# Attention and FFN on one core: k and v loaded in tiles of tokens 8 apart, sums of the first batch from the factors, numerators in two banks

## The chip, the core and the metric

The kernel runs on one core of a Trainium2 chip. The core has five engines that work side by side, each on a queue of its own, in order: TensorE (PE, matrix products; its weight loads are listed as PEld), VectorE (DVE), ScalarE (ACT), GpSimd (POOL) and SyncE (SP, which here only issues transfers). TensorE writes its results to PSUM, a memory of eight banks of 128 partitions x 512 float32; everything else lies in SBUF (128 partitions). Transfers to and from HBM run on 16 DMA engines; an engine issues one and later waits for its landing. The metric is the device time of one execution in microseconds (us), smaller is better: the median of several runs.

## The reference

Two parts, cut to what matters (batch 4, heads 4, sequence 1088, head_dim 32, r = 8, so 64 features; FFN of 128 x 2048 over 4352 tokens):

```python
def phi(x):
    a = np.einsum('rd,bhsd->bhsr', S1, x)
    b = np.einsum('rd,bhsd->bhsr', S2, x)
    return np.einsum('bhsi,bhsj->bhsij', a, b).reshape(*x.shape[:-1], r * r)
q_p, k_p = (phi(q), phi(k))
kv = np.einsum('bhsf,bhsd->bhfd', k_p, v)
z = np.sum(k_p, axis=2)
num = np.einsum('bhsf,bhfd->bhsd', q_p, kv)
den = np.einsum('bhsf,bhf->bhs', q_p, z)[..., None] + 1e-06
attn = (num / den)
...
x = attn.transpose(0, 2, 1, 3).reshape(B * S, H * D)
h = np.maximum(x @ w_in, 0.0)
out = h * h @ w_out
```

Each token has two sets of 8 factors, a and b; a feature is a product a_i b_j. The sum z of the features over the tokens can be had from the features (a column of ones beside v), or from the factors: the product of all a with all b over the tokens holds every sum of a_i b_j.

## The kernel before

The work is one long FFN with the attention of later batches woven in. The 1024 main tokens of a batch form two groups of 512 (four tiles of 128 each), and 64 tokens are left over ("rest"). So there are eight chunks of 512 tokens and one chunk of 256 rest tokens. A chunk passes through 16 blocks: `first_product` (line 892) multiplies a 128-column slice of w_in with xT into a `pg` bank (tag "pg", two banks), Relu and Square follow on VectorE and ScalarE (or ScalarE and GpSimd, or ScalarE alone), and `block` (973) multiplies the result with w_o into `po`. `store_gen` (862) turns `po` back, scales it with beta and writes it out. A float32 product is recorded as two instructions.

The order is written out by hand. Attention of batches 1 to 3 is made of generators in `lanes`, which `pump` advances after each block by block numbers and rough engine loads; `later` lists loads by block number. The first group of batch 0 has nothing to hide behind, and its code stands in order from line 1004 on:

- s_ps turns S1 and S2; w_bd is made of it on VectorE.
- `turned` (246) transposes 32x32 blocks of k and q on VectorE; `proj` (269) makes the factors of four tiles in TensorE (16 recorded instructions a tile group) and ScalarE copies them.
- `outer` (340) makes features from the factors, half of a group on VectorE, half on GpSimd.
- `Kv` (389) multiplies features of k with v and a column of ones, four heads a tile, into kv_ps; `finish` copies it to kvbd, the block-diagonal right side, with the sums in column 32 of each block.
- `turned_half` (1050) transposes features of q in TensorE (`t_ps`, tag "ms", two banks) and copies them to phTh; the second group's (phq1) go by `turn_features` directly: two tiles a time for both `t_ps`.
- `numerators` (527) multiplies them with kvbd into nd, one PSUM tile of two banks (tag "nd", one buffer); `normalize` (544, with parts=4) divides on VectorE and makes xs (float16); x_ps transposes xs to xT.
- `first_two` (931) issues the first two `pg`; the second group's numerators follow, then the gapless run of blocks.

`idle_products` (237) are products of zeros that keep TensorE going in its waits. Batches 1 to 3 have their sums from the factors already (`KvRows`, 428), with constants made in a lane (`sum_constants`, 220).

Loads are issued from SP in the order of lines 164 to 184; k of batch 0 by group (`load_k`, 95), v by head (`load_v`, 121, one a head), v's rest in two. In SBUF partition 32h + j of k holds 34 neighbouring tokens of head h; the transposes write with a stride of four so that tile t has every token of its place.

Of the kernel before, what the change touches and what calls it, by code (L numbers as in the profile page):

```python
# [21 lines left out]
def kernel(  # L22
# [32 lines left out]
    Identity = mybir.ActivationFunctionType.Identity  # L55
# [33 lines left out]
    def load_all(t, src, b):  # L89
        sp.dma_start(  # L90
            t[:, :],
            bass.AP(src.tensor, src.offset + b * H * S * D, [[NM * D, 128], [1, NM * D]]),
        )

    def load_k(b, g):
        sp.dma_start(
            _v(k_sb[b], 128 * g, [[256, 4], [1, 128]]),
            bass.AP(
                k.tensor,
                k.offset + b * H * S * D + 128 * g,  # L100
                [[NM * D, 128], [256, 4], [1, 128]],
            ),
        )
# [9 lines left out]
    def load_rest(t, src, b):  # L113
        sp.dma_start(
            t[:, 1024:1088],
            bass.AP(
                src.tensor, src.offset + b * H * S * D + 1024, [[NM * D, 128], [1, 64]]
            ),
        )

    def load_v(b, h, eng):
        eng.dma_start(
            v_sb[b][:, 256 * h : 256 * h + 256],
            bass.AP(
                v.tensor,
                v.offset + (b * H + h) * S * D,
                [[NM * D, 32], [8 * D, 4], [1, 256]],
            ),
        )

    def load_v_rest(b, i, eng):
        eng.dma_start(
            _v(v_rm[b // 2], 0, [[D, H], [1, D]], 64 * (b % 2) + 32 * i, 32),
            bass.AP(
                v.tensor,
                v.offset + (b * H * S + 32 + i) * D,
                [[NM * D, 32], [S * D, H], [1, D]],
            ),
        )
# [25 lines left out]
    load_k(0, 0)  # L165
    load_k(0, 1)
    load_rest(k_sb[0], k, 0)
    load_q(0, 0)
    for i in range(4):
        load_v(0, i, sp)  # L170
    load_q(0, 1)
    for i in range(2):
        load_v_rest(0, i, sp)
# [3 lines left out]
    load_all(k_sb[1], k, 1)  # L177
    load_w_o(1)
    for i in range(4):
        load_v(1, i, sp)  # L180
    for i in range(2):
        load_v_rest(1, i, sp)
    load_all(q_sb[1], q, 1)
    load_rest(q_sb[0], q, 0)


# [5 lines left out]
    eps = cpool.tile([128, 1], F32)  # L192
    dve.memset(eps[:], 1e-6)
# [26 lines left out]
    def sum_constants():  # L220
        yield 1, 0
        dve.tensor_reduce(
            out=pick_s[:, :], in_=_v(iden, 0, [[1, 32], [32, 4]]), axis=AX, op=add
        )
        yield 1, 0
        pool.tensor_copy(
            out=_v(pick, 0, [[8, 32], [1, 8]]), in_=_v(pick_s, 0, [[1, 32], [0, 8]])
        )
        dve.tensor_reduce(
            out=_v(own_j, 0, [[8, 2], [1, 8]]),  # L230
            in_=_v(iden, 0, [[64, 2], [1, 8], [8, 8]]),
            axis=AX,
            op=add,
        )

# [10 lines left out]
    def turned(x, g, of_q=False):  # L246

        if g < 2:
            xt = apool.tile([128, 512], F32, tag="xt", bufs=6)
            c0, w = (512 * g, 128) if of_q else (128 * g, 256)  # L250
            dve.transpose(  # L251
                _v(xt, 0, [[128, 4], [1, 4], [4, 32]]), _v(x, c0, [[32, 4], [w, 4], [1, 32]])
            )
        else:
            xt = apool.tile([128, 64], F32, tag="xtr", bufs=4)
            if of_q:
                dve.transpose(_v(xt, 0, [[1, 2], [2, 32]]), _v(x, 1024, [[32, 2], [1, 32]]))
            else:
                dve.transpose(xt[:, :], x[:, 1024:1088])
# [9 lines left out]
    def proj(xt, ps_tag="ms"):  # L269
# [5 lines left out]
        act.copy(ab[:, :], ab_ps[:, :])  # L275
# [64 lines left out]
    def outer(ph, ab, t0, m, eng, a=None, g=None):  # L340


        if g is None:
            a, b, n, c0, c1 = ab if a is None else a, ab, 16, 64 * t0, 64 * t0 + 8
        else:
            a, b, n, c0, c1 = ab, ab, 8, 128 * g + 32 * t0, 256 + 128 * g + 32 * t0
        eng.tensor_tensor(  # L347
            out=_v(ph, 256 * t0, [[64, 4 * m], [8, 8], [1, 8]]),
            in0=_v(a, c0, [[n, 4 * m], [1, 8], [0, 8]]),
            in1=_v(b, c1, [[n, 4 * m], [0, 8], [1, 8]]),  # L350
# [37 lines left out]

    class Kv:

        def __init__(self, b):
            self.b, self.n = b, 0
            self.ps = pspool.tile([128, 512], F32, name="kv_ps", tag="nd", bufs=1)

        def products(self, ph, c0, vt, v0, v1, one, p0=0, n=128):
            z = 64
            for h in range(H):
                off = v0 + v1 * h
                for f in range(0, 64, z):
                    x = 64 * (h % 2) + f  # L400
                    nc.tensor.matmul(  # L401
                        self.ps[x : x + z, 64 * (h // 2) : 64 * (h // 2) + 64],
                        ph[p0 : p0 + n, c0 + 64 * h + f : c0 + 64 * h + f + z],
                        _v(vt, off, [[one - off, 2], [1, D]], p0, n),
                        start=self.n == 0 and h < 2,
                        stop=False,
                        skip_group_check=True,
                    )
            self.n += 1

        def tiles(self, ph, g, ts):
            for t in ts:
                self.products(ph, 256 * t, v_sb[self.b], D * (4 * g + t), 256, VONE)

        def rest(self):
            r, p0 = self.b // 2, 64 * (self.b % 2)
            self.products(rest_ab[r][1], 0, v_rm[r], 0, D, H * D, p0, 64)

        def finish(self, engs):
            u = self.b  # L420
            for x in range(2):
                evict(
                    engs[x],
                    _v(kvbd[u], VW * x, [[2 * VW, 2], [1, VW]], 64 * x, 64),
# [729 lines left out]
```

## Time and profile before

| what | value |
| --- | --- |
| runs | 198.64, 198.82, 198.88 us; median 198.82 |
| the profiled execution | 199.0 us, of it the span of the trace 197.2 us |
| VectorE, ScalarE, GpSimd busy | 61%, 57%, 32% of the span |
| a block (`pg` and the two passes of `po`) | starts 1.07 us apart |
| transfers | 21.91 MB, mean 111 GB/s, over 300 GB/s from 9.3 to 20.6 us |
| k transposes of batch 0 | 3.90 to 6.01 us |
| first kv product | 9.29 us |
| first numerators of group 0 | 13.90 us |
| first `pg` / first `po` | 19.04 / 21.09 us |

The span runs from the first to the last instruction of the trace; the run's time has some 1.8 us more around it. In the rows of a timeline the columns are start, length (both us), engine, line, operation, output<-inputs, shapes and count; in brackets stands the engine's idle time before it and what ended it. In a row of a stage the columns are the stage, its length, and the busy time and number of instructions of PE, PEld, DVE, ACT and POOL, then granted clock, DMA share and GB/s.

### The profile page before, as it was taken

The page shows a single profiled execution, that of the slowest core. Times are in us where ns is not written, and L with a number is a line of the kernel's source. Part 1 is how long each engine was busy: PE and PEld are TensorE (multiplying, and loading weights), DVE is VectorE, ACT ScalarE, POOL GpSimd, SP SyncE. Part 2 cuts the span into 40 slices and gives each one's busy share as a digit, 9 for nine tenths or more (in the row PEclk, how much of TensorE's full clock was granted, in tenths as well). Part 3 has the DMA queues.
Part 4 walks back from the last instruction along what each step waited for, and adds up shares of the span by engine and source line. Part 5 has one row for each costly group of instructions (what it writes and reads, how often), then busy time and mean ns, then how long its engine had stood idle before and what let it go on. Part 6 is the DMA issues. An engine that isn't in the chain of part 4 may idle for free.

```text
span 197.2 us, 3669 instructions
## 1 busy us (share of the span) xinstructions
PE 191.5 (97%) x1402; PEld 102.7 (52%) x1402; DVE 120.5 (61%) x264; ACT 112.5 (57%) x221; POOL 64.0 (32%) x84
## 2 busy tenths in 40 slices
PE   7999999999999999999999999999999999999992
PEld 2784544555545454555554645455545444544791
DVE  4837897565587738547977264556387545545671
ACT  3235767663666666464757474557466656565570
POOL 3604224635245018241632271516313222222000
PEclk9999999999999999999999999999999999999999
DMA  5799840395990105982000159721000100100011
GB/s 159 217 341 326 279 128 2 83 269 165 267 327 34 56 3 130 294 240 99 2 5 0 55 118 303 193 98 53 2 0 3 53 0 0 53 0 2 0 57 27
DMA packets 13634, 21.91 MB, mean 111 GB/s; under 512 B 2672, under 2 KB 8048, under 8 KB 13616
## 3 DMA queue, kind: packets, MB, share of 16 engines
q1 hardware_dynamic: 13376, 21.60, 36.6%
q8 instruction: 11, 0.18, 0.4%
q10 hardware_dynamic: 240, 0.07, 0.2%
q14 instruction: 7, 0.06, 0.1%
HBM read 15.61 MB, written 6.06 MB: 110 GB/s over the span
## 4 chain that ended last, share of the span: by engine, by line
PE 94%; DMA 2%; DVE 1%; issue 1%; ACT 0%
PE po L994 56%; PE pg L906 16%; PE nd L265 5%; PE ab_ps L265 3%; PE kvr_ps L438 2%; PE po L953 2%; PE o_ps L871 2%; PE po_r L953 2%; DMA k_sb<-in_k_dram 2%; PE kv_ps L401 1%; PE x_ps L617 1%; PE ab_ps L282 1%; PE t_ps L1042 1%; PE idle_ps L240 1%; PE abr_ps L265 0%
## 5 line engine op out<-in xcount | busy, mean ns | idle before, releaser
L994 PE MATMUL po<-g,w_o 128*128 128x512 f32 x256 | 130.6, 592 | 0.0
L923 DVE TENSOR_SCALAR gt<-pg 128x512 f32<-128x512 f32 (+1 forms) x107 | 69.2, 651 | 52.5 <-PE pg L906 38.1
L926 ACT ACTIVATE g<-gt 128x512 f32<-128x512 f32 (+1 forms) x107 | 63.8, 598 | 58.8 <-DVE gt L923 56.4
L994 PEld LDWEIGHTS po<-g,w_o 128*128 128x128 f32 x256 | 48.5, 191 | 35.7 <-issue 19.2
L914 POOL TENSOR_TENSOR g<-gt 128x512 f32<-128x512 f32 x23 | 23.9, 1040 | 79.3 <-ACT gt L913 79.3
L906 PE MATMUL pg<-xT,w_in 128*128 128x512 f16 x126 | 47.8, 380 | 0.0
L906 PEld LDWEIGHTS <-w_in 128*128 128x128 f16 x142 | 13.8, 98 | 25.0 <-issue 24.1
L332 POOL TENSOR_TENSOR phF<-f,f 128x576 f32<-128x576 f32 (+1 forms) x12 | 16.1, 1364 | 12.8 <-DMA f<-q_two 12.8
L347 POOL TENSOR_TENSOR ph_k<-ab 128x512 f32<-128x512 f32 x14 | 14.5, 1070 | 10.1 <-ACT ab L288 8.8
L913 ACT ACTIVATE gt<-pg 128x512 f32<-128x512 f32 x23 | 13.4, 581 | 0.0
L879 DVE TENSOR_TENSOR o_sb<-o_ps,beta 128x512 f32<-128x512 f32 x8 | 5.5, 692 | 6.9 <-PE o_ps L871 6.9
L251 DVE STREAM_TRANSPOSE xt<-k_sb 128x512 f32<-128x512 f32 x8 | 8.6, 1117 | 1.7 <-DMA k_sb<-in_k_dram 1.7
L265 PEld LDWEIGHTS nd<-kvbd,phF 128*64 128x64 f32 x208 | 6.9, 137 | 4.5 <-issue 4.5
L251 DVE STREAM_TRANSPOSE xt<-q_sb 128x512 f32<-128x512 f32 x8 | 8.6, 1121 | 0.0
L265 PEld LDWEIGHTS ab_ps<-w_bd,xt 128*64 128x64 f32 x160 | 7.1, 163 | 2.5 <-issue 1.2
L265 PE MATMUL ab_ps<-w_bd,xt 128*64 128x64 f32 x160 | 7.5, 252 | 0.4 <-DVE w_bd L1008 0.4
L920 ACT ACTIVATE g<-gt 128x512 f32<-128x512 f32 x12 | 7.6, 630 | 0.4
L240 PE MATMUL idle_ps<-zero 128*128 128x512 f16 x17 | 6.6, 511 | 1.2 <-DVE own L198 1.2
L265 PE MATMUL nd<-kvbd,phF 128*64 128x66 f32 x208 | 7.7, 224 | 0.0
L919 ACT ACTIVATE gt<-pg 128x512 f32<-128x512 f32 x12 | 7.0, 587 | 0.0
L953 PE MATMUL po<-w_o,g 128*128 128x128 f32 x32 | 6.2, 278 | 0.0
L953 PE MATMUL po_r<-w_o,g 128*128 128x128 f32 x32 | 6.0, 275 | 0.0
(114 smaller groups left out, 143.4 us busy)
## 6 DMA issues: line engine op xcount, KB each, us to landing
q_two<-qf SPq DMA_DIRECT2D x8, 288.0 KB, 4.1
f<-q_one SPq DMA_DIRECT2D x4, 576.0 KB, 6.1
f<-q_two SPq DMA_DIRECT2D x4, 576.0 KB, 4.7
v_sb<-in_v_dram SPq DMA_DIRECT2D x16, 128.0 KB, 4.0
out_dram<-o_sb SPq DMA_DIRECT2D x8, 256.0 KB, 2.4
k_sb<-in_k_dram SPq DMA_DIRECT2D x3, 544.0 KB, 6.1
q_sb<-in_q_dram SPq DMA_DIRECT2D x3, 544.0 KB, 4.4
w_in<-in_moe_w_in_dram SPq DMA_DIRECT2D x2, 512.0 KB, 6.2
```

The source lines that it names most:

```text
L240: nc.tensor.matmul(idle_ps[:, :], zero[:, 0:128], zero[:, :])
L251: dve.transpose(_v(xt, 0, [[128, 4], [1, 4], [4, 32]]), _v(x, c0, [[32, 4], [w, 4], [1, 32]]))
L265: nc.tensor.matmul(out_ps[p0 + c : p0 + c + z, c0 : c0 + w], lhsT[:, l0 + c : l0 + c + z], rhs)
L332: pool.tensor_tensor(out=ph[:, c], in0=fs[g][0][:, c], in1=fs[g][1][:, c], op=mult)
L347: eng.tensor_tensor(out=_v(ph, 256 * t0, [[64, 4 * m], [8, 8], [1, 8]]), in0=_v(a, c0, [[n, 4 * m], [1, 8], [0, 8]]), in1=_v(b, c1, [[n, 4 ...
L906: nc.tensor.matmul(pg[:, 0:nt], w_in[:, 128 * c : 128 * c + 128], xT[:, 0:nt])
L913: act.activation(gt[:, 0:nt], pg[:, 0:nt], Relu)
L914: pool.tensor_tensor(out=g2[:, 0:nt], in0=gt[:, 0:nt], in1=gt[:, 0:nt], op=mult)
L923: dve.tensor_scalar(out=gt[:, 0:nt], in0=pg[:, 0:nt], scalar1=0.0, scalar2=None, op0=amax)
L926: act.activation(g2[:, 0:nt], gt[:, 0:nt], Square)
L953: nc.tensor.matmul(po[r][:, 0:128], g2[:, 128 * r : 128 * r + 128], w_o[:, 128 * c : 128 * c + 128], start=c == 0, stop=c == NC - 1,)
L994: nc.tensor.matmul(po[0][:, 0:nt], w_o[:, 128 * c : 128 * c + 128], g2[:, 0:nt], start=(c == 0), stop=(c == NC - 1),)
```

## The change

*Loads.* k lies by head: partition 32h + j holds, for t = 0 to 3, the tokens 256t + 8j to 256t + 8j + 7 of head h. That is one load a head into 32 partitions (for batch 0 the fourth from ScalarE's queue), and one for the rest. v is one load a batch, its rest one. The transposes then write contiguously, and a tile's tokens are 8 apart. A chunk's rows are written out by four transfers of 32 partitions instead of one of 128.

*Sums of batch 0.* The column of ones is gone from `Kv`; `factor_sums` multiplies the factors, ScalarE copies the result (kvz), `pick_sums` and `own_sums` bring it into kvbd, as `KvRows` did for the others. The constants are made at the start.

*Order and numerators.* w_bd comes before the k transposes; an idle product stands between the two projections of k. All eight q transposes follow the kv products. The first group's numerators go to two tiles (nd and nd_b, the latter with the tag "pg"), with the second group's projection between. `normalize_first` takes both: ScalarE copies the fourth tile's numerators (num_last), VectorE makes three tiles of xs, GpSimd the fourth. The second group's features are turned in two halves, its second half and the numerators of it behind `first_two`; the last numerators come in a lane (`second_half`), behind the second `po`. ScalarE converts w_in in 2 + 2 pieces, not 3 + 1.

Cut to its core:

```diff
-    def load_k(b, g):
-        sp.dma_start(
-            _v(k_sb[b], 128 * g, [[256, 4], [1, 128]]),
+    def load_k(b, h, eng):
+        eng.dma_start(
+            _v(k_sb[b], 0, [[256, 4], [1, 256]], 32 * h, 32),
             bass.AP(
                 k.tensor,
-                k.offset + b * H * S * D + 128 * g,
-                [[NM * D, 128], [256, 4], [1, 128]],
+                k.offset + (b * H + h) * S * D,
+                [[8 * D, 32], [256 * D, 4], [1, 8 * D]],
             ),
+        )
...
+    def load_v(b):
+        sp.dma_start(
+            _v(v_sb[b], 0, [[256, H], [1, 256]]),
             bass.AP(
+                v.tensor, v.offset + b * H * S * D, [[8 * D, 128], [S * D, H], [1, 8 * D]]
             ),
         )
...
-    load_k(0, 0)
-    load_k(0, 1)
-    load_rest(k_sb[0], k, 0)
+    for h in range(H):
+        load_k(0, h, act if h == 3 else sp)
+    load_k_rest(0)
     load_q(0, 0)
-    for i in range(4):
-        load_v(0, i, sp)
+    load_v(0)
...
+    def factor_sums(ps, c0, ab, a0, a1, w, p0, n, first, last):
+
+        nc.tensor.matmul(
+            ps[32 * w : 32 * w + 32, c0 : c0 + 32],
+            ab[p0 : p0 + n, a0 : a0 + 32],
+            ab[p0 : p0 + n, a0 + a1 : a0 + a1 + 32],
+            start=first,
+            stop=last,
+        )
...
             for h in range(H):
-                off = v0 + v1 * h
-                for f in range(0, 64, z):
-                    x = 64 * (h % 2) + f
...
+                x = 64 * (h % 2)
+                nc.tensor.matmul(
+                    self.ps[x : x + 64, D * (h // 2) : D * (h // 2) + D],
+                    ph[p0 : p0 + n, c0 + 64 * h : c0 + 64 * h + 64],
+                    vt[p0 : p0 + n, v0 + v1 * h : v0 + v1 * h + D],
...
+    def normalize_first(nds, xT):
...
+        act.copy(_v(last, 0, [[32, 4], [1, 32]]), _v(nds[1], 256, [[VW, 4], [1, 32]]))
+        for i, nd in enumerate(nds):
+            dve.tensor_reduce(
+                out=_v(top, 8 * i, [[4, 2], [1, 4]]),
+                in_=_v(nd, 0, [[256, 2], [VW, 4], [1, 32]]),
+                axis=AX, op=amax, apply_absolute_value=True,
+            )
+            dve.tensor_scalar(
+                out=den[:, 8 * i : 8 * i + 8], in0=_v(nd, D, [[256, 2], [VW, 4]]),
+                scalar1=1e-6, scalar2=None, op0=add,
+            )
...
+        for t in range(3):
+            dve.scalar_tensor_tensor(
+                out=_v(xs, 128 * t, [[32, 4], [1, 32]]),
+                in0=_v(nds[t // 2], 256 * (t % 2), [[VW, 4], [1, 32]]),
...
+        pool.tensor_tensor(
+            out=_v(xs, 384, [[32, 4], [1, 32]]),
+            in0=_v(last, 0, [[32, 4], [1, 32]]),
+            in1=_v(rs, 12, [[1, 4], [0, 32]]),
+            op=mult,
+        )
...
-        sp.dma_start(dst, o_sb[:, :])
+        for dst, p0, n, c0, w in dsts:
+            sp.dma_start(dst, _v(o_sb, c0, [[1, w]], p0, n))
...
-    xk = [turned(k_sb[0], 0)]
     dve.tensor_tensor(
         out=_v(w_bd, 0, [[16, H], [1, 16]]),
...
+    xk = [turned(k_sb[0], 0), turned(k_sb[0], 1)]
...
+    pk = [proj(xk[0], "pg")]
+    idle_products(1)
+    pk.append(proj(xk[1], "pg"))
...
+    for g in range(2):
+        for t in range(4):
+            factor_sums(kv0.ps, 512, pk[g][1], 32 * t, 128, t, 0, 128, g == 0, g == 1 and t > 0)
+    factor_sums(kv0.ps, 512, rest_ab[0][0], 0, 32, 0, 0, 64, False, True)
+    sums = apool.tile([128, 32], F32, name="kvz", tag="kvz")
+    act.copy(sums[:, :], kv0.ps[:, 512:544])
...
+    idle_products(2)
+    kv0.tiles(phk[0], 0, range(4))
+    zt_ps = pspool.tile([128, 32], F32, name="zt_ps", tag="po", bufs=2)
+    pick_sums(zt_ps, 0, sums)
+    own_sums(0, zt_ps, 0)
+    xq1 = turned(q_sb[0], 1, True)
...
-    kv0.tiles(phk[1], 1, range(4))
+    kv0.tiles(phk[1], 1, range(2))
     kv0.rest()
+    kv0.tiles(phk[1], 1, range(2, 4))
     kv0.finish((act, act))
-    turned_half(2, (act, dve))
+    pqT = [turned_half(phq, 0, (act, act)), turned_half(phq, 2, (act, dve))]
+    nd0 = [numerators(0, pqT[0], None, range(2))]
     pq1 = proj(xq1, "pg")
     phq1 = ph_tile("ph_q", 2)
     outer(phq1, pq1[1], 0, 2, pool)
-    nd0 = numerators(0, pqT)
+    nd_b = pspool.tile([128, 512], F32, name="nd_b", tag="pg", bufs=2)
+    nd0.append(numerators(0, pqT[1], nd_b, range(2, 4)))
     idle_products(2)
...
+    norm = normalize_first(nd0, xT0)
     next(norm)
+    outer(phq1, pq1[1], 2, 2, pool)
+    for c in range(2):
...
+    pqT = [turned_half(phq1, 0, (act, act))]
+    idle_products(4)
+    chunk_of(0, 0, xT0, next(norm))
     first_two()
-    nd1 = numerators(0, pqT1, True)
+    nd1 = numerators(0, pqT[0], None, range(2))
+    pqT.append(turned_half(phq1, 2, (act, dve)))
     nd_taken[0] = True
     for _ in range(2):
         first_product()
...
+    def second_half():
+        numerators(0, pqT[1], nd1[:, 512:1024], range(2, 4))
+        yield 1, 0
+        yield from x_gen(0, 1, None, (), nd1)
+
+    lanes.append([second_half(), 2, 1])
```

## The prediction

> **What bounds the kernel now.** I read the busy times and the chain of waits of the page first, then busy time by stage, then the timeline of the first 28 us, then the loads.
>
> ```profile
> PE 191.5 (97%) x1402; PEld 102.7 (52%) x1402; DVE 120.5 (61%) x264; ACT 112.5 (57%) x221; POOL 64.0 (32%) x84
> ...
> PE 94%; DMA 2%; DVE 1%; issue 1%; ACT 0%
> ```
>
> TensorE is busy for 191.5 of 197.2 us and is 94% of the chain that ended last. By stage:
>
> ```profile
> 14.90:20.64 5.74, 5.35 (x57) 2.86 (x53) 4.32 (x14) 3.65 (x8) 2.25 (x4) 1.00 1.00 327
> 20.64:190.00 169.36, 169.36 (x1137) 87.55 (x1134) 105.71 (x223) 102.48 (x198) 56.79 (x61) 1.00 0.33 96
> ```
>
> From 20.64 us on TensorE has no gap. Its order there is the same before and after, except for what the change pushes into the first blocks. So the question is when the gapless part begins and how much work it must hold. The opening, in order of time (idle time before a row stands in brackets):
>
> ```profile
> 3.90 1.09 DVE L251 STREAM_TRANSPOSE xt<-k_sb 128x512 f32<-128x512 f32 x1 [1.71 <-DMA k_sb<-in_k_dram]
> ...
> 5.09 2.10 PE L265 MATMUL ab_ps<-w_bd,xt 128*64 128x64 f32 x32 [0.41 <-DVE w_bd L1008]
> ...
> 9.29 1.36 PE L401 MATMUL kv_ps<-v_sb,ph_k 128*64 128x64 f32 x32
> ```
>
> The chain runs: first k load (lands at 3.87), transpose, projections, kv products, then the numerators, VectorE's normalisation, x transposes and the first `pg` at 19.04. Some rows of its end:
>
> ```profile
> 12.80 0.66 PE L1042 MATMUL t_ps<-iden,ph_q 128*128 128x128 f32 x4
> ...
> 13.90 0.42 DVE L77 COPY phTh<-t_ps 128x256 f32<-128x256 f32 x1 [2.68 <-ACT phTh L75]
> ...
> 18.40 0.60 PE L1042 MATMUL t_ps<-iden,ph_q 128*128 128x128 f32 x4
> ...
> 21.07 1.29 DVE L923 TENSOR_SCALAR gt<-pg 128x512 f32<-128x512 f32 x2 [0.74 <-PE pg L906]
> ```
>
> Two things matter here. VectorE's copy out of a `t_ps` starts only when ScalarE's copy from the same tile has ended (13.86): two engines' reads of one PSUM tile stand in line. And the four t_ps transposes at 18.40 lie in TensorE's wait for the first xT, so they cost nothing now.
>
> **The change, part by part.** Where I give "before -> after", the first is from the timeline, the second is my running sum.
>
> *Loads of k.* The first transpose reads all 128 partitions, so it now waits for all four head loads instead of the 256 KB of `load_k(0,0)`. The nearest row is the second k load, with which the same 512 KB are in:
>
> ```profile
> DMA to landing us min/median/max: 3.1/3.4/3.6
> ```
>
> It was issued at 1.22 and took 3.4: 4.6. Three issues on SP at about 0.5 each (v issues took 0.59 to 0.67, k issues 0.45 to 0.53) put the third head at 1.8 to 2.0; the fourth stands behind two s_nat issues on ScalarE, at 1.66. With the smallest landing of a 128 KB v load, 2.5, that is 4.4; with 3.6 it is 5.6. I take 4.8. Moving w_bd ahead of the transposes costs nothing, since s_ps is in at 4.14 and w_bd takes 0.20. The two reductions of the constants (0.34, 0.40) fit in VectorE's idle 1.71 before 3.90, the pick copy (0.40) in GpSimd's 3.0 before w_bt. Without that cover each would delay the w_bd line by its length.
>
> [...]
>
> *Projections to kv products.* Turned k at 4.8 + 1.06, TensorE starts at 5.9 (before 5.09). The pace is half in this stage: the idle products at 1.19 are 0.43 apart, those at 16.18 0.21. The 32 projections of k took 1.89 (5.09 to 6.98), so 0.95 to 6.85; the new idle product 0.43 to 7.28; second half 0.95, rest 0.12, q 1.06 (as 7.27 to 8.33): 9.4. The 18 new factor_sums instructions load 32-wide weights. Their pitch at full pace is in these rows of weight loads (first and last columns: start and length; one lasts 0.11 to 0.14):
>
> ```profile
> 120.86 0.49 PEld L438 LDWEIGHTS kvr_ps<-ph_k,v_sb 128*32 128x32 f32 x32 [0.76 <-issue]
> ...
> 123.59 0.32 PEld L485 LDWEIGHTS kvt_ps<-kvz,pick 128*64 128x64 f32 x8
> ```
>
> (0.49 - 0.11)/31 = 0.012 each, double at half pace: 0.2 to 0.45, I take 0.35, to 9.75. Two idle products, 0.43 to 0.86, take 0.6: kv starts at 10.35 (before 9.29). VectorE (k turned to 6.9, q to 8.25, first ph_k to 8.95) and GpSimd (ph_k to 8.4) are done by then, v is in (a 512 KB load issued near 3.3; the old last v quarter, issued at 4.83, landed 3.2 later). The kvz copy (0.19) ends about 10.15, under the idle products.
>
> *kv products.* 72 instructions, with 32 streamed columns instead of 64. The pick row above, 64-wide weights and 16 columns, still has a pitch of (0.32 - 0.138)/7 = 0.026; the numerators' loads (64-wide, 66 columns) have (1.02 - 0.137)/31 = 0.0285. Halving the columns should thus save next to nothing. Before, the two groups took 1.30 and 1.46; 72 x 0.0285 is 2.05. With 8 pick instructions (0.2) the bounds are 2.25 and 2.96, I take 2.6: end at 12.95. Before it was 12.80, but with an idle product and half of the t_ps transposes in between (10.59 to 11.34).
>
> *Turned q features and numerators.* All eight t_ps now follow: 2 x 0.53, to 14.0. ScalarE copies kvbd (0.43) and three phTh (0.375 each) from 13.1 to 14.72, VectorE's follows to 15.17. First numerators from 14.35, 0.5; projection 0.51; second bank 0.5: end at 15.85 (before 14.95).
>
> *Normalisation.* The first bank's reduction and den are hidden. ScalarE's copy num_last (0.26, as the 128x128 xT_rem copy) reads nd_b first, and VectorE's reduction stands behind it: 16.27, reduction 0.42, den 0.17: 16.9. From there to the first xs 1.02 as now (16.13 to 17.15), three xs of 0.28 instead of four, and 0.76 from the last xs to `pg` (18.28 to 19.04): 19.55. GpSimd's share of the fourth tile (0.20 and about 0.4, by the 256-wide product's 0.62) ends before the third xs. So `pg` is 0.5 late. Removing ScalarE's den (0.27) is in this sum.
>
> *After `pg`.* The second half of the next group's t_ps (0.53) and of its numerators (0.55) now stand behind the first two `pg`. The numerators were behind them before too; the transposes were not, so 0.53 enters the gapless part. And a new line forms, counted from `pg`: ScalarE Relu 0.62 to 1.22, Square to 1.86, its phTh to 2.23, VectorE's phTh behind it to 2.69, the next gt to 3.35. TensorE ends its first po at 2.86 and its next `pg` needs that gt's bank: a gap of 0.54. Before, that gt ended at 21.75 and the `pg` went at 22.01, so no gap. The second `pg` of the steady part, 4.04 behind the first one before (23.08), comes at 5.05: 1.0 more.
>
> *SP and the stores.* A store is four issues instead of one (0.54 to 0.64 each, 1.7 more). At 44.12 four factor transfers stand behind the store; the last, issued at 51.29, lands 4.0 to 6.2 later, so with 1.7 more by 59.2, GpSimd's two products (2.8) end at 62.0 and the numerators start at 61.96. Bound 0 to 0.1, I take 0. The last stores (186.40) end their issue before the rows at 193.36. Later k loads are five issues instead of one, v two instead of six: even.
>
> **Sum**: 0.5 + 1.0 = 1.5. The profiled execution took 199.0 (span 197.2 and 1.8 around it), so 200.5; against the median of 198.82 it is **200.3**. Taking the cheap end everywhere (loads 0.4, idle and sums 0.3, kv 0.35, num_last 0.3, no gap 0.54) gives -0.4; the dear end (loads 0.8, 0.36, 0.36) 3.0.
>
> **Rivals.** [...] *B, kv products cost by their columns*: they then halve, 1.0 less, 199.3. The pick row speaks against it. *C, not slower*: TensorE's full pace comes before the projections, at about 6 us rather than 9.5. Then they and the idle products shrink, and kv starts when VectorE's first ph_k ends, 8.85 instead of 10.35: all of the 1.5 is gone, 198.8. It decides only if TensorE counts as busy enough across its longer gap, now 4.69 to 5.9; the old gap, to 5.09, did not bring it. [...] *D, the change doesn't do what it says in time*: the two lines I see behind ScalarE do not cost what I charge, and the split pays: no gap after `pg` (0.54), num_last out of the way (0.3) and kv at its cheap end (0.35) leave 1.5 - 1.2 = 0.3: 199.1. For it: VectorE is busy for 4.32 of the 5.74 us up to 20.64, so it has some room; against: the wait for ScalarE in the row at 13.90.
>
> **Numbers.** Forecast 0.50 (199.6 to 201.2), A 0.18, B 0.12, C 0.12, D 0.08. Slower by over 0.2% (0.4 us, about what this measurement can tell from no change): forecast, A and B, 0.80. Within it: most of D, a third of C, 0.10; faster 0.10. Range 199.0 to 201.7: it leaves out the better half of C and D and the end of A.
>
> **What would show it.** First k transpose near 4.8 (5.4 or later: A); kv products from about 10.3 with a pitch of 0.028 (0.015: B); idle products 0.21 apart before 8 (C); num_last ahead of VectorE's second reduction; first `pg` near 19.5; VectorE's phTh behind ScalarE's, and a TensorE gap of about 0.5 behind the first po. No gap there, or a `pg` before 19, makes this wrong.

## The result, and the profile after

The changed kernel takes 200.87 us (median of 18 runs, 199.11 to 201.52) against 198.09 us for the kernel before (18 runs beside it, 197.51 to 199.30): a ratio of 1.011, 95% interval 1.0082 to 1.0138. The median of before in these runs lies 0.7 below that of the three runs shown ahead, which are the first three of the 18. The ratios here and below leave out executions more than 1.5% above the fastest of their kernel (two of `u_code`, one of `u_best`); the medians are over all runs.

The times of each kernel lie in two heaps. Before: 9 runs at 197.51 to 197.96, 9 at 198.22 to 199.30. After: 6 at 199.11 to 199.53, 12 at 200.40 to 201.52. The profiled execution of after belongs to the lower heap (199.53 us, span 197.7), that of before (199.0, span 197.2) to the upper. So the two traces show only 0.5 us between them, and what separates the heaps has to be found too. No execution of after from its upper heap was profiled; `a_order` and `a_bare` below stand in for it.

The page of after, busy times and the chain of waits:

```profile
PE 189.9 (96%) x1427; PEld 101.9 (52%) x1427; DVE 116.2 (59%) x267; ACT 113.0 (57%) x224; POOL 64.8 (33%) x86
...
PE 87%; DMA 7%; SPq 3%; DVE 0%; issue 0%
```

The chain now has 7% of loads and 3% of their issue. Read this with care: from the gt (Relu's output) at 21.12 us it goes back to a landing of q at 21.08, which that gt does not read; in the timeline below it stands right behind VectorE's phTh. Busy time by stage, cut where TensorE has its last gap:

```profile
14.90:21.86 6.96, 5.56 (x41) 2.83 (x40) 4.37 (x15) 3.81 (x10) 3.82 (x6) 1.00 1.15 281
21.86:190.00 168.14, 168.14 (x1140) 87.06 (x1140) 100.36 (x219) 102.24 (x197) 55.73 (x59) 1.00 0.36 96
```

The part without a gap begins at 21.86, not at 20.64. From the second `pg` of the steady part to the end of the span it is 174.12 us before (197.2 - 23.08) and 174.06 after (197.7 - 23.64). So the stores in four pieces, the later loads and all batches behind cost nothing that these traces show, and the whole difference arises in the first 24 us. The timeline of after there:

```profile
5.22 1.31 DVE L246 STREAM_TRANSPOSE xt<-k_sb 128x512 f32<-128x512 f32 x2 [0.60 <-DMA k_sb<-in_k_dram]
...
9.21 1.12 PE L429 MATMUL kv_ps<-v_sb,ph_k 128*64 128x32 f32 x32
...
15.15 0.42 DVE L553 TENSOR_REDUCE small<-nd_b 128x8 f32<-128x256 f32 x1 [0.73 <-ACT num_last L551]
...
18.49 0.59 PE L954 MATMUL pg<-xT,w_in 128*128 128x512 f16 x2 [0.47 <-DVE xT L76]
...
20.78 0.42 DVE L76 COPY phTh<-t_ps 128x256 f32<-128x256 f32 x1 [1.19 <-ACT phTh L74]
...
21.86 0.38 PE L924 MATMUL pg<-xT,w_in 128*128 128x512 f16 x1 [0.28 <-DVE gt L941]
```

k is turned 1.3 us later than before, but in 0.69 us a transpose, not 1.08. The first `pg` comes at 18.49, 0.55 earlier than before. Behind it VectorE's phTh waits for ScalarE's, and TensorE waits for the gt that stands behind it; the second steady `pg` follows 5.15 us after the first `pg` (4.04 before).

### The profile page after: what moved, and what is told of

It is laid out like the page before. It is cut to its first block, busy times and chain, and to the rows that moved or that the text cites. A ratio compares the mean times of both kernels' runs of the same rounds, so it can differ in the third digit from the quotient of the medians.

```text
span 197.7 us, 3769 instructions
## 1 busy us (share of the span) xinstructions
PE 189.9 (96%) x1427; PEld 101.9 (52%) x1427; DVE 116.2 (59%) x267; ACT 113.0 (57%) x224; POOL 64.8 (33%) x86
## 4 chain that ended last, share of the span: by engine, by line
PE 87%; DMA 7%; SPq 3%; DVE 0%; issue 0%
PE po L1012 55%; PE pg L924 15%; DMA w_o<-in_moe_w_out_dram 5%; PE nd L255 4%; PE kvr_ps L466 2%; PE po L971 2%; PE o_ps L888 2%; PE po_r L971 2%; PE ab_ps L255 2%; DMA q_sb<-in_q_dram 1%; PE ab_ps L274 1%; PE x_ps L632 1%; SPq L139 1%; SPq L89 1%; SPq L150 1%; SPq L115 0%
## 5 line engine op out<-in xcount | busy, mean ns | idle before, releaser
L342 POOL TENSOR_TENSOR ph_k<-ab 128x512 f32<-128x512 f32 x14 | 14.6, 1072 | 11.3 <-ACT ab L280 9.2
L255 PEld LDWEIGHTS ab_ps<-w_bd,xt 128*64 128x64 f32 x160 | 6.0, 137 | 3.0 <-DVE xt L246 1.6
L255 PE MATMUL ab_ps<-w_bd,xt 128*64 128x64 f32 x160 | 6.3, 224 | 1.3 <-DVE xt L246 1.3
L235 PE MATMUL idle_ps<-zero 128*128 128x512 f16 x16 | 5.8, 476 | 1.2 <-DVE own L199 1.2
L888 PEld LDWEIGHTS o_ps<-iden,oT 128*128 128x128 f32 x32 | 3.9, 140 | 3.9 <-issue 2.9
L246 DVE STREAM_TRANSPOSE xt<-k_sb 128x512 f32<-128x512 f32 x8 | 5.3, 690 | 0.6 <-DMA k_sb<-in_k_dram 0.6
```

Of the source, the lines that this page charges most:

```text
L255: nc.tensor.matmul(out_ps[p0 + c : p0 + c + z, c0 : c0 + w], lhsT[:, l0 + c : l0 + c + z], rhs)
L342: eng.tensor_tensor(out=_v(ph, 256 * t0, [[64, 4 * m], [8, 8], [1, 8]]), in0=_v(ab if a is None else a, c0, [[n, 4 * m], [1, 8], [0, 8]]), ...
L888: nc.tensor.transpose(o_ps[:, 128 * t : 128 * t + 128], oT[:, 128 * t : 128 * t + 128], iden[:, :])
```

## The experiments

The kernel before ran beside each group of experiments, with medians of 197.87, 198.68 and 197.94 us, by the share of its upper heap. So each run is compared by its ratio to the before beside it.

### What makes two heaps: the pace of TensorE at the opening

In the trace of after the idle product at 4.29 and the next one last 0.39, and 16 projections 0.69; in that of before the idle product at 4.08 lasts 0.61 and 16 projections 1.12 (at 7.27). The theory: TensorE starts at half pace, how soon it goes to full pace depends on how much work it has there, and the wait for k (from about 4.7 to 5.1 before, to 6.0 after) puts it off in some executions. Three kernels change only the products of zeros around s_ps. `a_fill4` (the changed kernel):

```diff
     nc.tensor.transpose(s_ps[:, :], s_nat[:, :], iden[0:16, 0:16])
-    idle_products(1)
+    idle_products(4)
```

> The changed kernel with four idle products instead of one between s_ps and the first projection of k, so that TensorE has work until about 5.9 us instead of 4.7. The changed kernel's 18 runs fall into two heaps, 199.1 to 199.5 (6 runs) and 200.4 to 201.5 (12), and its profiled execution, at 199.53, has full-pace products from 4.3 us on. Theory P (when TensorE reaches full pace is what parts the heaps, and the long wait 4.7 to 6.0 spoils the interval in which it would be reached): nearly all runs in one heap at 198.8 to 199.6, ratio to before 1.004 to 1.009. Rival L (the loads or something else parts them): both heaps remain, median 200.5 to 201.3, ratio 1.010 to 1.016.

`b_fill2` (the kernel before, same place):

```diff
-    idle_products(1)
+    idle_products(2)
```

> The kernel before with two idle products instead of one at the same place, which covers its wait of 0.4 us there (4.7 to 5.1). Its own runs lie at 197.5 to 198.0 and at 198.6 to 199.3. Theory P: nearly all runs at 197.5 to 198.1, ratio to before 0.996 to 0.999. Rival L: both heaps remain, ratio 1.000 to 1.002.

`a_bare` (the changed kernel):

```diff
-    idle_products(6)
+    idle_products(2)
...
-    idle_products(1)
```

> The changed kernel with two instead of six idle products at the start and none behind s_ps: TensorE has next to nothing to do before 5.99 us. Theory P: full pace always comes late, the low heap is gone and the runs lie at 200.4 to 202.0, ratio 1.013 to 1.020. Rival L: the same two heaps as the changed kernel, some runs at 199.1 to 199.6.

| kernel | runs | median (range) | ratio, 95% interval |
| --- | --- | --- | --- |
| before, beside them | 18 | 197.87 (197.69 to 199.20) | |
| b_fill2 | 12 | 197.81 (197.71 to 198.03) | 0.998 (0.9963 to 0.9998) |
| a_fill4 | 7 | 199.94 (199.36 to 200.07) | 1.0074 (1.0045 to 1.0103) |
| a_bare | 4 | 201.19 (200.94 to 201.32) | 1.0148 (1.0113 to 1.0182) |

One more product of zeros takes the upper heap of before away, three more that of after, and fewer products leave only the upper one. The timelines of `b_fill2` (first fence) and `a_bare` (second) show the two paces:

```profile
4.08 1.03 PE L240 MATMUL idle_ps<-zero 128*128 128x512 f16 x2
5.08 1.67 PE L265 MATMUL ab_ps<-w_bd,xt 128*64 128x64 f32 x32
```

```profile
5.95 1.12 PE L255 MATMUL ab_ps<-w_bd,xt 128*64 128x64 f32 x16 [1.44 <-DVE xt L246]
7.01 0.61 PE L235 MATMUL idle_ps<-zero 128*128 128x512 f16 x1
```

32 projections take 1.67 in `b_fill2`, where the pace changes among them, and 16 take 1.12 in `a_bare`. The theory stands: each edit of the products alone moved the heaps as it says. Of `a_fill4` the ratio is as expected, but its median lies 0.34 above the expected range and 0.5 above the lower heap of after; a section below shows a wait of its own. Nor is the time of the change fixed by it: with 4 products `a_fill4` takes 3.87 us from the first k transpose to the kv products (5.57 to 9.44), no longer than after at full pace (3.99), while in `u_code` the first 16 projections still take 1.02 (from 6.18; 0.69 at full pace in after).

`b_fill2` is better than both kernels, and with `a_fill4` it gives the price of the change with little of this chance: 2.1 us (199.94 - 197.81; second steady `pg` at 22.10 and 24.20).

### k's loads: the order of the heads

`a_order` is the changed kernel with another order of the loads, `t_order` the same with the 4 products of zeros, `u_best` the same in the kernel `u_code` below.

```diff
-    for h in range(H):
+    for h in (0, 2, 1, 3):
         load_k(0, h, act if h == 3 else sp)
```

> The changed kernel with its three SP loads of k in the order head 0, 2, 1 (head 3 stays with ScalarE). In the profile of the changed kernel heads 0 and 1 landed 2.4 us after their issue, heads 2 and 3 took 3.5 and 3.2, and the first transpose began at 5.22. [...] Rival I (the last load issued is late because the queue behind it, k's rest and q, shares the engines): first transpose again at 5.1 to 5.3, whichever head is third.

> The changed kernel with 4 products of zeros behind s_ps (as in a_fill4, whose median was 199.94 us), and SP loading k's heads in the order 0, 2, 1. Theory A (a head's load into 32 partitions runs slower beside the load into the neighbouring 32): the first k transpose starts at 4.7 to 5.0 us instead of 5.2 to 5.6, everything up to the first `pg` moves with it, first `pg` at 18.3 to 18.6 (a_fill4: 19.04), median 199.1 to 199.5. Rival (q's load is late next, the path before the kv products does not move): first transpose earlier, but first kv product still at 9.4, median 199.8 to 200.1.

In the trace of after the first two head loads land 2.4 us after their issue, the third 3.5, the fourth 3.2; in `a_order` the third and fourth take 3.0 and 2.7. The timeline of `a_order`:

```profile
4.72 1.31 DVE L246 STREAM_TRANSPOSE xt<-k_sb 128x512 f32<-128x512 f32 x2 [0.32 <-DMA k_sb<-in_k_dram]
```

With the order 0, 2, 1 the first transpose starts at 4.72, 5.05 and 4.99 (`a_order`, `t_order`, `u_best`); with 0, 1, 2 in eight traces at 5.03 to 5.57, mean 5.28. So the order is worth some 0.35 us of k's landing, though the ranges touch. The third load takes 3.0 to 3.3 us in the three traces with 0, 2, 1 and 3.5 to 3.8 in `after`, `u_code` and `a_fill4`. In either order it takes longer than the first two (2.3 to 2.5), so the order is only part of it, and what else holds the third load stays open. `a_order` took 200.84 (2 runs, 200.74 and 200.93, ratio 1.0131), too few to be told from after. `t_order` took 199.58 (12 runs, 199.02 to 201.09; ratio 1.0046, 1.0024 to 1.0068), just above the theory's range and below the rival's; its trace reached the kv products at 9.41, no earlier than `a_fill4` (9.44): from the first k transpose to there it took 4.36 us, `a_fill4` 3.87. So a gain in time is not shown; an earlier start of the kv products shows only in `u_best` (below), and there in part by the pace.

### Behind the first `pg`

`t_gt` is `a_fill4` with

```diff
-    pqT.append(turned_half(phq1, 2, (act, dve)))
+    pqT.append(turned_half(phq1, 2, (act, act)))
```

`t_early` is `t_gt` with the four transposes ahead of x_ps (`turned_half` cut into `turned_in`, the transposes, and `turned_out`, the copies):

```diff
     outer(phq1, pq1[1], 0, 2, pool)
+    outer(phq1, pq1[1], 2, 2, pool)
     nd_b = pspool.tile([128, 512], F32, name="nd_b", tag="pg", bufs=2)
...
-    outer(phq1, pq1[1], 2, 2, pool)
...
-    idle_products(4)
+    t_last = turned_in(phq1, 2)
+    idle_products(2)
     chunk_of(0, 0, xT0, next(norm))
...
+    pqT.append(turned_out(t_last, (act, act)))
```

> a_fill4 with both phTh of the second group's second half copied by ScalarE (VectorE had one of them). Theory (VectorE's phTh, which starts only behind ScalarE's, holds gt2 and so the second `pg` behind `first_two`): VectorE idles no 1.2 us, the 0.28 us gap ahead of that `pg` goes, the second steady `pg` comes 0.25 to 0.5 us earlier after the first `pg` (a_fill4: 5.16 after it), median 199.4 to 199.7 against 199.94. Rival (TensorE's own work, t_ps and two pieces of numerators, sets it): same within 0.1, 199.85 to 200.05.

> a_fill4 with the second half's t_ps transposes of the second group put ahead of x_ps in the place of two of the four products of zeros (its features issued to GpSimd ahead of its share of xs), and both phTh of it by ScalarE. Theory (what stands behind the first `pg` that stood ahead of it before costs its own length): second steady `pg` 0.5 earlier by the transposes and 0.3 to 0.5 by phTh, 4.0 to 4.4 after the first `pg` (5.16 in a_fill4), the first `pg` up to 0.15 later by GpSimd; median 199.0 to 199.3. Rival (the gapless run starts when VectorE and ScalarE can keep up, not when TensorE is free): 4.7 to 5.2 after the first `pg`, median 199.7 to 200.0.

`t_gt`: 199.25 (12 runs, 198.68 to 199.64; ratio 1.0023, 1.0003 to 1.0044), below the range of the theory. Its timeline has no gap there any more, and the second steady `pg` comes 4.71 after the first, 0.45 less than in `a_fill4` (5.16):

```profile
20.72 1.02 PE L1012 MATMUL po<-g,w_o 128*128 128x512 f32 x2
21.57 0.38 PE L924 MATMUL pg<-xT,w_in 128*128 128x512 f16 x1
```

`t_early`: 199.84 (12 runs, 199.42 to 201.45; ratio 1.0068, 1.0043 to 1.0094), slower than `t_gt`. Two reasons, in its timeline:

```profile
15.10 2.10 POOL L342 TENSOR_TENSOR ph_q<-ab 128x512 f32<-128x512 f32 x2 [4.85 <-ACT ab L265]
...
16.23 0.98 DVE L532 TENSOR_TENSOR small<-small,small 128x16 f32<-128x16 f32 x1
```

```profile
21.38 1.13 PE L1012 MATMUL po<-g,w_o 128*128 128x512 f32 x2
```

VectorE's product of 128x16 takes 0.98 us (0.17 or 0.18 in the other traces, 0.26 in `t_last`): it ends when GpSimd's second features end (17.20), and the first `pg`, counted from the kv products, is late by 0.8. And the move itself returns little: the second steady `pg` comes 4.57 after the first, 0.14 better than in `t_gt`. The first po stands 1.82 behind `pg`, right behind ScalarE's Square (to 21.33) and 0.66 behind the second pair of `pg`; in `t_gt` it stands at 2.07, 0.44 behind that pair. So without the transposes TensorE has a wait there, which they partly filled. Before, all numerators filled it; now half of them come behind the second po, where nothing waits, and take 0.62 (22.74 to 23.36 in `t_gt`). So the theory fell (it gave 4.0 to 4.4), and the rival holds in part. By this reckoning what costs the 0.5 to 0.7 that are left against before (4.57 and 4.71 against 4.04) is the numerators that moved out, more than the transposes that moved in; no run moved the numerators back, so this is argued and not shown.

### The copy num_last

`t_last` is `a_fill4` without it:

```diff
-        act.copy(_v(last, 0, [[32, 4], [1, 32]]), _v(nds[1], 256, [[VW, 4], [1, 32]]))
...
-        for t in range(3):
+        for t in range(4):
             dve.scalar_tensor_tensor(
...
-        pool.tensor_tensor(
-            out=_v(xs, 384, [[32, 4], [1, 32]]),
```

> a_fill4 with num_last undone: VectorE makes all four tiles of xs from PSUM, ScalarE copies nothing, GpSimd has no share. Theory (the copy of num_last runs ahead of VectorE's second reduction of the same tile and holds it 0.27 us, which is what the fourth tile costs on VectorE, 0.3): the second reduction starts 0.2 to 0.3 earlier, xs ends at about the same time, first `pg` within 0.1 of a_fill4's 19.04, median 199.8 to 200.05. Rival (the split to three engines is worth its 0.3): 0.2 to 0.35 slower, 200.15 to 200.3. Rival (it costs more than it brings): 199.6 to 199.75.

199.53 (12 runs, 199.18 to 200.61; ratio 1.0059, 1.0035 to 1.0083). From the first product into nd_b to the end of xs it takes 3.54 us (14.76 to 18.30), with the copy 3.50 (`a_fill4`: 14.40 to 17.90). The reduction starts 0.30 earlier and the fourth tile takes 0.26: in the trace the split brings what it costs. The median lies under all three ranges, 0.4 below that of `a_fill4`, but beside another before; the intervals of the two ratios overlap, and single executions of these kernels differ by more, for the reason that follows. So this rests on the two traces.

### A wait that no engine explains: TensorE's own instructions

In `t_order`, whose profiled execution was the longest of its 12 (201.09), TensorE stands still ahead of the second group's first t_ps. From its timeline:

```profile
15.03 1.07 POOL L342 TENSOR_TENSOR ph_q<-ab 128x512 f32<-128x512 f32 x1 [4.68 <-ACT ab L265]
16.15 0.14 PEld L1071 LDWEIGHTS t_ps<-iden,ph_q 128*128 128x128 f32 x1 [1.10 <-POOL ph_q L342]
...
17.81 0.38 PE L1071 MATMUL t_ps<-iden,ph_q 128*128 128x128 f32 x2 [2.27 <-POOL xs L576]
```

The features end at 16.10 and the weights of the transpose are loaded at 16.15, so its wait is over. Its product starts at 17.81; the engine named there (xs) is no input of it. What fits is a packet of the instruction queue. Of the 0.2 us from 14.8 in `t_order`:

```profile
q1 hardware_dynamic: 49, 0.03, 96.6%
q8 instruction: 1, 0.02, 47.8%
```

There are 11 such packets of 16 KB in the trace. TensorE has 2,860 recorded instructions in it, VectorE, the next, 267 in after; so the packets are taken to be TensorE's, an estimate from these counts. In the traces with such a wait TensorE goes on 2.65 to 3.0 us behind the start of this packet (read in steps of 0.2 us): `t_gt` 13.6 and 16.25, `a_fill4` 14.0 and 16.78, `t_early` 14.2 and 16.98, `t_last` 14.6 and 17.30, `t_order` 14.8 and 17.81. The wait beyond GpSimd's end is 0.2, 0.65, 0.8, 0.8 and 1.7 us. VectorE's chain to xs covers its first 0.3: from the kv products to the first `pg` it is 9.27 us in `t_gt`, 9.60 in `a_fill4`, 9.76 in `t_last` and 10.66 in `t_order`. The traces of after, `a_order` and `a_bare` show no such wait (t_ps 0.06 behind the features in after): with 3 or more products less ahead, the 221st product, where the test below finds the wait, comes later there. Two kernels test it by the count of TensorE's instructions alone. `u_code` is `t_gt` with fewer:

```diff
     outer(phq, pq[1], 3, 1, pool)
-    idle_products(2)
...
     nd0.append(numerators(0, pqT[1], nd_b, range(2, 4)))
-    idle_products(2)
...
     pqT = [turned_half(phq1, 0, (act, act))]
-    idle_products(4)
```

`u_shift` is `t_gt` with more, in a wait for k:

```diff
     idle_products(4)
+    tiny = pspool.tile([128, 512], F32, name="tiny", tag="po", bufs=2)
+    for i in range(24):
+        nc.tensor.matmul(tiny[0:32, 0:32], zero[:, 0:32], zero[:, 0:32])
```

> t_gt (a_fill4 with both last phTh by ScalarE) without the 2 products of zeros ahead of the kv products, the 2 behind the last numerators and the 4 ahead of x_ps: 8 products and 8 weight loads less ahead of the first `pg`. Theory F (TensorE's third block of instructions comes late from HBM beside the loads: its packet starts at 13.0 to 15.2 us in ten traces, TensorE goes on 2.65 to 3.0 us later, and with a_fill4's count of instructions the block begins with the first group-1 t_ps): the block now begins 8 products later, at x_ps or the first `pg`; t_ps starts as soon as GpSimd has its features (within 0.15 us of their end at 16.1), first `pg` at 18.1 to 18.7, the runs lie closer together, median 198.6 to 199.0 against t_gt's 199.25. Rival (GpSimd's signal is late, whatever TensorE's count): t_ps starts 0.1 to 1.7 us behind the features, median 199.1 to 199.4. Rival (the products of zeros kept the pace up here): projections or transposes at half pace, median over 199.5.

> t_gt with 24 products of zeros of 128x32 (about 0.3 to 0.7 us) behind the 4 behind s_ps, in a wait for k. Theory F: the third block of instructions begins 24 products earlier, inside the group-1 projection or the last numerators (index 194 to 200 of the old count, 13.9 to 14.4 us); TensorE stands still there for 0.5 to 2 us with no releaser that fits, and the wait ahead of t_ps is gone or is only GpSimd's; everything behind is later, median 199.6 to 200.8 against t_gt's 199.25. Rival (GpSimd's signal is late, whatever TensorE's count): no wait between the projection and the last numerators, time as t_gt, 199.0 to 199.4.

`u_shift`: 200.05 (8 runs, 199.72 to 200.56; ratio 1.0083, 1.0054 to 1.0112). The wait has moved into the middle of the projection, where one product has all that the next one has:

```profile
14.08 0.51 PE L255 MATMUL ab_ps<-w_bd,xt 128*64 128x64 f32 x11
...
14.79 0.39 PE L255 MATMUL ab_ps<-w_bd,xt 128*64 128x64 f32 x5 [0.20 <-issue]
```

"issue" says that the engine waited for nothing that the profile shows. 221 recorded products stand ahead of this wait; in `a_fill4` and `t_order` it was 220, and there the weights of the next had been loaded. The packet began at 12.0, 2.8 us before the products go on. The 16 projections take 1.10, not `t_gt`'s 0.63: 0.47 lost, slightly less than the 0.5 to 2 expected. And GpSimd's share of the wait ahead of t_ps is all that is left there (product at 16.79, features to 16.73). The kv products also started 0.2 later (9.59 against 9.38), which makes the rest of the 0.67 by which the second steady `pg` is late.

The kernel before has fewer products ahead (209 to the first `pg` in `b_fill2`, 232 in `a_fill4`): its 221st lies in the numerators behind that `pg` (18.58 to 19.74, packet at 13.6). In the three traces of that kernel's kind (before, `b_fill2`, `t_plain`) it is not late. So the change, with the 4 products, has moved TensorE's 221st product from about 18.9 to 16 us, where the transfers move less. In 15.00 to 17.00 us, `b_fill2` first, then `t_gt` (the last two columns are the share of DMA time and GB/s):

```profile
15.00:17.00 2.00, 1.84 (x11) 0.77 (x9) 1.83 (x10) 0.90 (x2) 1.00 (x2) 1.00 1.07 348
```

```profile
15.00:17.00 2.00, 1.26 (x8) 0.76 (x8) 1.48 (x8) 1.37 (x4) 1.06 (x1) 1.00 1.20 197
```

So the wait follows TensorE's count of instructions, which `u_shift` shows; that the packet is what it waits for is inferred from the times, and that the loads make the packet late was not tried: the rows above are all there is.

`u_code`: 199.35 (12 runs, 198.62 to 202.53; ratio 1.0058, 1.0024 to 1.0091). In its trace t_ps starts 0.05 behind the features, and the first `pg` comes at 18.70, as the theory says. But the median lies in the range of the first rival, and the runs lie farther apart, not closer. `u_best` shows why.

> u_code with SP loading k's heads in the order 0, 2, 1. Theory A: first k transpose at 4.7 to 5.0 us, the kv products and all up to the first `pg` 0.2 to 0.5 us earlier than in u_code, median 198.2 to 198.6. Rival (the time up to the kv products hangs on the pace of TensorE and on the features, not on k): the same as u_code within 0.1.

199.54 (12 runs, 198.28 to 202.04; ratio 1.0053, 1.0022 to 1.0084). That is above the theory's range. Its trace (200.01) reaches the kv products 0.67 and the first `pg` 0.68 earlier than that of `u_code` (9.42 and 18.70). Of this 0.43 stands at the first projection, by k (5.75 against 6.18), the rest comes from the pace (16 projections in 0.69 against 1.02). It loses it at once:

```profile
8.75 1.12 PE L429 MATMUL kv_ps<-v_sb,ph_k 128*64 128x32 f32 x32 [0.28 <-ACT kvz L1055]
...
18.02 1.01 PE L954 MATMUL pg<-xT,w_in 128*128 128x512 f16 x2 [0.48 <-DVE xT L76]
```

```profile
18.00:20.00 2.00, 1.98 (x18) 1.08 (x18) 0.69 (x1) 0.93 (x2) 0.49 (x2) 0.50 0.92 297
```

Two `pg` take 1.01 instead of 0.59, and the granted clock is 0.50 from 18 to 20 us (0.71 from 20 to 22). Without the products of zeros TensorE works 1.46 of the 3.68 us from 14.34 to 18.02. The trace of `u_code` has the same stretch (15.02 to 18.70, 1.46 of 3.68) and keeps its pace:

```profile
18.70 0.59 PE L954 MATMUL pg<-xT,w_in 128*128 128x512 f16 x2 [0.48 <-DVE xT L76]
```

So such a stretch puts the pace at risk and does not always cost it. The mean granted clock of each execution says which it was. Six of `u_best`'s runs lie at 198.28 to 199.10 with a clock of 0.999 or 1.000, six at 199.98 to 202.04 with 0.979 to 0.991. In `u_code` seven lie at 198.62 to 199.43 (0.999 or 1.000) and five at 200.10 to 202.53 (0.979 to 0.991); with the products, in `t_gt`, all 12 have 0.995 or more. So the products that were taken out had kept the pace, which was the second rival of `u_code`. The seven runs that kept it have a median of 198.94, inside the theory's range.

### What a strided write costs

`t_plain` is `b_fill2` with

```diff
-                _v(xt, 0, [[128, 4], [1, 4], [4, 32]]), _v(x, c0, [[32, 4], [w, 4], [1, 32]])
+                _v(xt, 0, [[128, 4], [32, 4], [1, 32]]), _v(x, c0, [[32, 4], [w, 4], [1, 32]])
```

> b_fill2 with the 128x512 transposes of k and q written contiguously instead of with a stride of four (the tiles then hold other tokens, beside v's unchanged ones, so the output is another; the work is the same). Theory (the strided write is what makes a transpose 1.06 to 1.11 us instead of 0.69 to 0.71, and the changed kernel gets that back): each transpose 0.66 to 0.72, q's projection starts 0.5 to 1.0 earlier (7.37 in b_fill2), kv products at 7.6 to 8.1 (8.52), median 197.0 to 197.5 against b_fill2's 197.81. Rival (hidden behind GpSimd's features or v's landing): transposes shorter, kv products at 8.3 to 8.6, median 197.6 to 197.9. Rival (the float32 transposes of the changed kernel are shorter for another reason, such as k's place in SBUF): transposes still 1.06.

197.50 (12 runs, 197.24 to 197.89; ratio 0.9952, 0.9929 to 0.9975). Timeline:

```profile
3.92 0.71 DVE L251 STREAM_TRANSPOSE xt<-k_sb 128x512 f32<-128x512 f32 x1 [1.73 <-DMA k_sb<-in_k_dram]
...
7.98 1.55 PE L401 MATMUL kv_ps<-v_sb,ph_k 128*64 128x64 f32 x32
```

0.71 instead of 1.08: the stride is the cause. The kv products start 0.54 earlier, inside the theory's range. But they take 1.55 instead of 1.15, since their weight loads wait 0.42 for GpSimd's features (6.54 to 8.63, against 6.64 to 8.73 in `b_fill2`), and the first `pg` is only 0.14 earlier (17.92). So the theory is right up to the start of the kv products, with a median at the edge of its range, and behind that the first rival's mechanism hides most of the gain.

## Why the prediction was right, step by step

The direction and the forecast case were right; the median lies 0.57 above the forecast and within both ranges. Part of that is luck. The medians differ by 2.78 us, where 1.5 was forecast. Upper heap against upper heap it is 2.23 (medians 201.10 and 198.87), lower against lower 1.63 (199.40 and 197.77); the rest comes from the upper heap's share, 12 of 18 executions against 9 of 18. The forecast was added to 198.82, a time of the upper heap, and met a median of the upper heap; nothing in it gave these shares.

By its own sign ("a `pg` before 19") the trace of after, with `pg` at 18.49, speaks against the forecast. That execution is of the lower heap, where the pace is that of rival C. The forecast reckoned with half pace up to the kv products, and the two traces of that kind test it: `a_order` (200.74) and `a_bare` (201.12), whose times are those of the upper heap. `a_order`, where k was turned at 4.72 (forecast 4.8): kv products 10.43 (10.35), first `pg` 19.70 (19.55), second steady `pg` 24.86 (24.60). `a_bare`, with the changed kernel's own load order, 5.19, 10.82, 20.10 and 25.25: from k on 0.4 to 0.65 late. **The mis-sized term is k's landing**: 4.8 was taken, 5.28 is the mean first transpose of the eight traces, 0.48 later. No run shows a mechanism of the loads that would bear A's chance of 0.18 and its part in the range; what the runs showed in its place is a first transpose at A's sign of 5.4 or later in three of the eight (5.41, 5.50, 5.57), and a third load that takes 3.0 to 3.3 us in one order of the heads and 3.5 to 3.8 in the other.

*From k to the kv products* two errors of like size cancel, as the timeline of `a_order` shows:

```profile
5.49 1.12 PE L255 MATMUL ab_ps<-w_bd,xt 128*64 128x64 f32 x16 [0.81 <-DVE xt L246]
...
9.20 0.44 PE L386 MATMUL kv_ps<-ab 128*32 128x32 f32 x16
...
10.43 1.12 PE L429 MATMUL kv_ps<-v_sb,ph_k 128*64 128x32 f32 x32
```

"Turned k at 4.8 + 1.06" took the row of before; contiguous output makes it 0.67 to 0.71 (all 16 in after), and TensorE starts 0.41 earlier than forecast (5.49 against 5.9). The projections with their idle product take 0.21 more than forecast (3.71 against 3.5), and the 18 factor_sums instructions 0.62 (9.20 to 9.82), not 0.35, beyond the bounds of 0.2 to 0.45. So the kv products' start, 0.08 off, is right by luck. That k's strided write was dear before, and that the change undoes it, was not in the forecast.

*kv products.* Forecast from kv's start to its end 2.6, measured 2.77 in after (9.21 to 11.98), with the pick products in it. 32 instructions of 32 columns take 0.96, 0.030 each; 32 of 64 columns took 1.09 in `b_fill2` (8.52 to 9.61), 0.034 each. Halving the columns saved next to nothing, and B is out.

*Numerators and num_last.* VectorE's second reduction does stand behind ScalarE's copy. From the kv start to the first `pg` the forecast has 9.20; `a_order` has 9.27, after 9.28. But the experiments show what this view could not: the split of the last tile brings no more than it costs (`t_last`), and the wait at TensorE's 221st product, which no row of before announced, added up to 1.4 us in the kernels with the 4 products (10.66 in `t_order` against 9.27), and nothing in the traces of after, `a_order` and `a_bare`.

*After `pg`.* Forecast 5.05 from the first to the second steady `pg`, measured 5.15 to 5.16. The gap was given as 0.54 and is 0.28 in the trace, since po ends later than reckoned (+3.08, not +2.86); the `pg` behind it comes at +3.37, where it was forecast. Undoing VectorE's share gave 0.45. "0.53 enters the gapless part" is right in size; by `t_early` what pays is rather the numerators that left TensorE's wait for Square, which no run tested by itself.

*SP and the stores* cost nothing in the traces, as forecast.

*Rivals.* C, with a chance of 0.12, happened in part: full pace came before the projections in the one execution of the lower heap (6 of 18 runs) that was profiled, and there the kv products started at 9.21. It was not worth the whole 1.5, since k was later than 4.8 and the part after `pg` stayed. The reasoning against it, that the longer gap would not bring full pace, holds for most runs and not for all. D is out: the gap is there.

Where the time went, then, with full pace ahead of the kv products in both (the traces of `a_fill4` and `b_fill2`, 2.1 us; from the first k transpose to the kv products 3.87 us in `a_fill4`, 3.99 at full pace in after; 32 projections 1.67 in `b_fill2`, 2.10 in before): 0.92 up to the kv products (k lands later, first transpose at 5.57, the latest of the eight, and its transposes gain some of it back), 0.06 from there to the first `pg` (9.54 and 9.60: 0.26 gained by the new order, as 9.28 in after shows, and 0.32 lost in that execution to the wait at the 221st product), 1.12 behind it. In the upper heap the pace comes on top: half speed through the opening, and for longer than before (projections at half pace up to 9.20 in `a_order`, to 8.33 in before).

## What to carry to other kernels

Before judging a change to an opening, make its pace certain: one product of zeros more in the first wait of the kernel before brought the range of its times from 1.5 us to 0.3, and was the only edit here that beat both kernels with the same result computed. When an engine waits and the releaser named is no input of the waiting instruction, look at the instruction queue's packets and count instructions; 24 short ones more moved such a wait to another place, where it cost 0.47 us (`u_shift`). Work behind a first product is free only as far as it fills a wait that stays: taking the transposes out gave back 0.14 of their 0.5 us (`t_early`), since the wait did not end with them.

## What the runs showed of the hardware

- TensorE lost its full pace after 3.7 us in which it worked 40% (0.85 us of 14 to 16 and 0.89 of 16 to 18, `u_best`: two `pg` then take 1.01), and kept it over an equal stretch in `u_code` (0.59); after a gap of 2.27 it kept it too in `t_order` (two t_ps products in 0.38). The fall in `u_best` is recorded as a granted clock of 0.50 (18 to 20 us); the half pace at the opening of before is recorded as 1.00 (0 to 5 us), and only the durations show it (0.61 against 0.39 in after for the same product).
- TensorE went on after a wait at its 221st product 2.65 to 3.0 us behind the start of an instruction packet of 16 KB, with transfers at 225 (`t_order`) and 226 GB/s (`t_gt`) from 13 to 15 us; that it waited for this packet is inferred.
- A 128x512 float32 transpose in blocks of 32x32 on VectorE takes 0.67 to 0.71 us with contiguous output (all 16 in after; 0.71 for the first in `t_plain`) and 1.06 to 1.18 with a stride of four (all 16 in before).
- A VectorE product of two small SBUF operands ended with a GpSimd product beside it: 0.98 us instead of 0.18 (`t_early`).
